# w_out's and w_ch's pieces decoded as one sequence, v's copies issued by ScalarE, x's rows stored two ticks later, and attention's state sums as one scan

## The chip, the cores and the metric

The kernel runs on one core of one Trainium2 chip. The metric is the device time of one execution in microseconds, the median of three runs. In the profile PE is TensorE (its weight loads are PEld), DVE is VectorE, ACT is ScalarE, POOL is GpSimd and SP is SyncE, which issues nearly all DMAs of this kernel.

## What is computed

A retention block (attention with a decay in place of the softmax), a block with a spatial gate, and a channel block follow one another. Cut to what matters:

```python
# q, k, v: (4, 8, 576, 64)
rel = pos[:, None] - pos[None, :]
Dmat = np.where(rel >= 0, gamma[:, None, None] ** rel[None, :, :], 0.0)
x = np.matmul(scale * np.matmul(q, k.transpose(0, 1, 3, 2)) * Dmat, v)   # heads side by side: (4, 576, 512)

h = gelu(x @ w_in)                                     # tanh form; w_in (512, 1024)
u, v = h[..., :512], h[..., 512:]
v_n = (v - mean(v)) / np.sqrt(var(v) + 1e-06) * g_ln
v_s = np.einsum('ts,bsd->btd', w_sg, v_n) + b_sg[None, :, None]
y = x + (u * v_s) @ w_out

xn = (y - mean(y)) / np.sqrt(var(y) + 1e-06) * g_ln2
out = y + np.maximum(xn @ w_ch1, 0.0) @ w_ch2          # w_ch1 (512, 2048), w_ch2 (2048, 512)
```

w_in, w_out and w_ch arrive as float64 words and are turned into float32 on the chip.

## The kernel before

The program is written out in one order; each engine carries out its own instructions in that order, and waits for the others by semaphores. Three stages follow one another.

**Attention** works on sixteen units, one for each of 4 batches and 4 pairs of heads, and is linear in the sequence: it is cut into four chunks of 128 positions and a rest of 64. For a unit, `scores` makes the products of q and k within the chunks (L224) and VectorE masks them (L229, L237); `states` (L239) makes a 64x64 state for each chunk and head (L245), side by side in one PSUM bank `us`, and sums them with decay: y of chunk c is y of chunk c - 1 times a factor per partition, plus the state. ScalarE copies chunk 0 (L251), and VectorE adds the other three one after another (L253). `attend` multiplies the masked scores with v (L277) and the summed states with q (L284, L290), with y as the stationary operand, and VectorE scales the result into `xb` (L295, L300). The loop (L453) puts scores and states of unit n + 1 ahead of attend of unit n. The tables of masks and decays, `tab`, one for each pair of heads, hold 451 columns and are loaded by SyncE between the first units; the factor is one column of it, at O_GC.

**Decoding in the background.** `f64_pieces` (L349) turns a list of 512-word pieces into float32. It loads two pieces ahead; then each piece takes four steps: a third load and a shift on VectorE (L142); the next VectorE instruction (L146), and the split of the piece before by ScalarE and GpSimd (L310, L311); a square on ScalarE (L148) and a VectorE instruction (L149); and the last VectorE instruction (L151), which waits for that square, with a store (L376) for w_ch. The steps are called by hand, `background(n)` for n steps: three in each attention unit from the third on, and then by the table `PACE`, so many after each tile. `background_steps` (L417) strings w_in, w_sg, w_out and most of w_ch together. w_out and w_ch are two calls of `f64_pieces`, so between them stands one step of its own: the last split of w_out and the first two loads of w_ch. By the counts of the table it is the second of three steps behind the first u chunk of batch 0.

**The gated stage** runs batch by batch. For each batch: `v_tile` makes 128 rows of v (in batches 0 and 2 also a tile numbered 4 that holds the rests of two batches), `u_chunk` four chunks of u in two halves, `sg_chunk` the spatial product with w_sg, whose five products over rows take v's tiles 0, 1, 2, 3 and the rest in this order, and `w_out_tile` the last product. Each evacuation by GELU on ScalarE (L529) is a tick, as is each half of the spatial product and each output tile. `after(n, fn)` puts work n ticks later into the program. So a tile of v is normalized in pieces over four ticks: mean and squares (L513, L514), variance and root (L498, L499), three small VectorE instructions (L519, L521, L523), and in the fourth the normalization on ScalarE (L526) with the split into high and low parts by ScalarE (L554) and GpSimd (L555). For the tile with the two rests, the fourth tick has DMAs in place of the split: two copy its lower half into `v_rest` (L587), a third puts the upper half over the lower (L588), and the split comes three ticks later. SyncE issues them. In batch 0 that fourth tick is the first half of the first u chunk, and tile 3's three small instructions come in the first half of the second. The splits of tiles 1, 2, the rests and 3 follow in this order.

Ahead of each u chunk, `turn_x` (L665) transposes 128 rows of x on VectorE into a tile of the pool `t` (five slots, shared with v's tiles and the rows that come back) and at once stores it with four DMAs on SyncE (L676); a fifth, shorter one comes ahead of the spatial product. `load_x` reads the rows back for the output tiles.

**The channel stage** (from L971 on) is a fast matrix product by blocks; it and the transformation of its weights are as they were.

Of the kernel before, what the change touches and what calls it, by code (L numbers as in the profile page):

```python
# [3 lines left out]

# [1 line left out]

# [5 lines left out]
F32 = mybir.dt.float32  # L12
# [3 lines left out]
ALU = mybir.AluOpType  # L16
# [3 lines left out]
B, H, S, D = 4, 8, 576, 64  # L20
E = H * D
NP = H // 2
F1 = 1024
F2 = 2048
C = 128
NC = S // C
R = S - NC * C
KE = E // 128
NF = F2 // 128
# [17 lines left out]
LATE = 6  # L47
# [15 lines left out]
O_GROW = O_MASKR + R  # L63
O_GK = O_GROW + C
O_GC = O_GK + 2
TA = O_GC + 1


O_GLN = 0
# [5 lines left out]
def const_tables():  # L75
    g = np.array(GAMMA, np.float64)
    p = np.arange(128)
    tab = np.zeros((NP, 128, TA), np.float64)
    for hp in range(NP):
        for h in range(2):  # L80
            gh = g[2 * hp + h]
            tab[hp, :, O_MASK + h * C:O_MASK + (h + 1) * C] = (np.arange(C)[None, :] >= p[:, None]) * gh ** -p[:, None]
            tab[hp, :, O_GK + h] = gh ** (C - p)
        gp = g[2 * hp + p // D][:, None]
        tab[hp, :, O_MASKR:O_MASKR + R] = (np.arange(R)[None, :] >= (p % R)[:, None]) * gp ** -(p % R)[:, None]
        tab[hp, :, O_GROW:O_GROW + C] = gp ** np.arange(C)[None, :] / np.sqrt(D)
        tab[hp, :, O_GC] = gp[:, 0] ** C
    return tab.astype(np.float32)


# [1 line left out]
def kernel(  # L92
# [12 lines left out]
    nc = tc.nc  # L105
    ctx.enter_context(tc.manual_schedule())
    act, dve, pool, pe = nc.scalar, nc.vector, nc.gpsimd, nc.tensor
# [12 lines left out]
    def col(t, o, n=1):  # L120
        return t[:, o:o + n]
# [9 lines left out]
    def f64_words(src, n):  # L131

        raw = f64_at[0].tile([128, n, 2], U32, tag="raw", name="raw")
        nc.sync.dma_start(out=raw.rearrange("p n w -> p (n w)"), in_=src.bitcast(U32))
        return raw

    def f64_to_f32(raw, n):


        c = f64_at[1].tile([128, n], U32, tag="c", name="c")  # L140
        w0, w1 = raw[:, :, 0], raw[:, :, 1]
        dve.tensor_scalar(  # L142
            out=c, in0=w1, scalar1=3, scalar2=0x3FFFFFFF, op0=ALU.logical_shift_left, op1=ALU.bitwise_and
        )
        yield
        dve.scalar_tensor_tensor(out=c, in0=w1, scalar=0xC0000000, in1=c, op0=ALU.bitwise_and, op1=ALU.bitwise_or)  # L146
        yield
        act.activation(out=f(w1), in_=f(w1), func=ACTF.Square)  # L148
        dve.scalar_tensor_tensor(out=c, in0=w0, scalar=29, in1=c, op0=ALU.logical_shift_right, op1=ALU.bitwise_or)  # L149
        yield  # L150
        dve.scalar_tensor_tensor(  # L151
            out=f(c), in0=f(w1), scalar=F64_LEAST ** 2, in1=f(c), op0=ALU.is_ge, op1=ALU.mult
        )
        return f(c)
# [4 lines left out]
    def bank():  # L159

        return banks.popleft()
# [3 lines left out]
    def slot(name):  # L165
        return wts.tile([128, 4 * 512], F32R, tag="w", bufs=9, name=name)
# [7 lines left out]
    pa = es_a.enter_context(tc.tile_pool(name="pa", bufs=2))  # L174

    tab = [pa.tile([128, TA], F32, tag=f"tab{hp}", bufs=1, name=f"tab{hp}") for hp in range(NP)]

# [61 lines left out]
    def states(n):  # L239
        u = units[n]  # L240
        us = bank()
        for c in range(NC):
            for h in range(2):
                r = slice(h * D, (h + 1) * D)
                pe.matmul(  # L245
                    us[r, c * D:(c + 1) * D], u["k"][:, c, r],
                    u["v"][:, c * C + h * D:c * C + (h + 1) * D], start=True, stop=True,
                )

        y = u["y"] = pa.tile([128, NC, D], F32, tag="y", name="y")  # L250
        act.copy(y[:, 0], us[:, 0:D])  # L251
        for c in range(1, NC):
            dve.scalar_tensor_tensor(  # L253
                out=y[:, c], in0=y[:, c - 1], scalar=col(tab[n % NP], O_GC), in1=us[:, c * D:(c + 1) * D],
                op0=ALU.mult, op1=ALU.add,
            )
        free(us)

    def attend_rest(n):
# [49 lines left out]
    def split(hi, lo, src):  # L309
        act.copy(hi, src)  # L310
        pool.tensor_tensor(out=lo, in0=src, in1=f(hi), op=ALU.subtract)  # L311

    def load_w_in():
        for k in range(KE):
            t = slot("w_in").rearrange("p (a n) -> p a n", a=2)
            wi.append(t)
            for x in range(0, F1, 512):
                c = slice(x, x + 512)
                yield (w_in[k, :, c], t[:, 0, c], t[:, 1, c])

    def load_w_out():
        for k in range(KE):
            if k % 2 == 0:
                s = slot("w_out").rearrange("p (k a n) -> p k a n", k=2, a=2)
            t = s[:, k % 2]
            wo.append(t)
            yield (w_out[k], t[:, 0], t[:, 1])
# [21 lines left out]
    def f64_pieces(pieces, lead=2):  # L349

        pieces = iter(pieces)
        ahead = deque()

        def load():
            todo = next(pieces, None)
            if todo is not None:
                ahead.append((todo, f64_words(todo[0], 512)))

        for _ in range(lead):
            load()  # L360
        yield
        before = None
        while ahead:
            load()
            todo, raw = ahead.popleft()
            steps = f64_to_f32(raw, 512)
            next(steps)
            yield
            if before is not None:
                split(*before)  # L370
                before = None
            c = yield from steps
            if len(todo) == 3:
                before = (todo[1], todo[2], c)
            else:
                nc.sync.dma_start(out=todo[1], in_=c)  # L376
            yield
        if before is not None:
            split(*before)
# [35 lines left out]
    w_ch_pieces = decode_w_ch()  # L415

    def background_steps():  # L417
        yield from f64_pieces(load_w_in(), 1)
        yield from load_w_sg()
        yield from f64_pieces(load_w_out())  # L420
        yield from f64_pieces(islice(w_ch_pieces, 2 * NF - LATE))

    bg = background_steps()

# [114 lines left out]
    def after(n, fn):  # L539
        late.append((step[0] + n, fn))  # L540
# [16 lines left out]
    def v_tile(b, i, ps=None):  # L557

        if ps is None:
            ps = v_products(b, i)  # L560
        if i == 0:
            vn[b] = tuple(big.tile([128, NC + 1, 512], F32R, tag=f"vn{a}", name=f"vn{a}") for a in "hl")
            if b % 2:
                after(1, lambda: iter([split_v(b, NC, v_rest[b])]))
        t = t1.tile([128, 512], F32, tag="t", bufs=NBT, name="t")

        st = numbers(t1)

        def norm_t():
            yield from squares(st, t, vn[b][0][:, i])  # L570

            def numbers_t():
                root(st, st[:, 1:2], 1.0 / 512, 1e-6)
                yield

            after(1, numbers_t)
            after(2, lambda: newton(st))

            def rest():
                normed(t, st)  # L580
                if i < NC:
                    split_v(b, i, t)
                else:

                    r = v_rest[b + 1] = t1.tile([128, 512], F32, tag="rest", bufs=1, name="v_rest")
                    for h in range(2):
                        nc.sync.dma_start(out=r[h * R:(h + 1) * R], in_=t[R:])  # L587
                    nc.sync.dma_start(out=t[R:], in_=t[0:R])  # L588
                    after(3, lambda: iter([split_v(b, i, t)]))
                yield  # L590

            after(3, rest)

        gelu(t, ps, ps, norm_t, st[:, 0:1])
        background(int(PACE[b][0][i]))
# [69 lines left out]
    def turn_x(b, i):  # L665

        n = 128 if i < NC else R
        t = t1.tile([128, 512], F32, tag="t", bufs=NBT, name="x_t")[:, 0:4 * n]
        dve.transpose(  # L669
            out=t.rearrange("p (q k c) -> p k q c", k=KE, c=32),  # L670
            in_=xb[b][:, :, i * 128:i * 128 + n].rearrange("p k (q c) -> p k q c", c=32),
        )
        at = 0 if i < NC else b % 2 * R
        to = x_dram[y_rows.index((b if i < NC else b | 1, i)), at:at + n]
        for q in range(4):
            nc.sync.dma_start(  # L676
                out=to[:, q * 128:(q + 1) * 128].rearrange("(a j) c -> j a c", j=32),
                in_=t[q * 32:(q + 1) * 32].rearrange("j (a c) -> j a c", c=128),
            )

    def load_x(b, i):
        x_rows[b, i] = t1.tile([128, E], F32, tag="t", bufs=NBT, name="x_r")
# [152 lines left out]
    for b in range(B):  # L835
# [27 lines left out]
        if last:  # L863
            for _ in bg:
                pass
            t = [wts.tile([128, KE * (S + R)], F32R, tag="xt", bufs=2, name="fe") for _ in range(2)]
            u = [slot("fe") for _ in range(4)]
# [36 lines left out]
        if last:  # L904
            next(feat)
            w1_at = [[slot("w1") for _ in range(2)]]
            t = slot("w2").rearrange("p (i a n) -> p i a n", i=2, a=2)
# [254 lines left out]
```

## Time and profile before

| | before |
|---|---|
| median of 3 runs | 700.74 us (699.19 to 702.92) |
| profiled execution: time, span | 702.03 us, 700.2 us |
| TensorE busy | 668.7 us (96%) |
| VectorE busy | 482.9 us (69%) |
| ScalarE busy | 303.2 us (43%) |
| GpSimd busy | 341.7 us (49%) |
| TensorE's granted clock, mean | 0.986 |
| DMA | 116.96 MB, mean 167 GB/s |

The span reaches from the first to the last instruction; the profiled execution's own time is 1.8 us more. Busy times are shares of the whole span and say nothing of a stage: attention lies in the first 90 us, the gated stage between 85 and 330 us, the channel stage behind it. A matmul is pipelined, so that the busy time of TensorE counts overlapped matmuls once. [...]

### The profile page before, as it was taken

How to read it: one execution, taken by the hardware profiler on the slowest of the kernel's cores; microseconds unless marked ns; L12 is line 12 of the kernel's file. 1: busy time of each engine (PE TensorE's matmuls, PEld its weight loads, DVE VectorE, ACT ScalarE, POOL GpSimd, SP SyncE). 2: the span in 40 equal slices, each digit the busy share in tenths (PEclk: the TensorE clock that was granted, in tenths of full speed). 3: DMA queues.
4: the chain of work that ended last, by engine and by line, in shares of the span. 5: the costliest groups of instructions: out<-in, count | busy, mean ns of one | idle time of the engine just before them, and what ended most of it. 6: DMA issues, size and time to landing. Idle time of an engine off the chain costs nothing.

```text
span 700.2 us, 11668 instructions
## 1 busy us (share of the span) xinstructions
PE 668.7 (96%) x4294; PEld 594.4 (85%) x4294; DVE 482.9 (69%) x925; ACT 303.2 (43%) x584; POOL 341.7 (49%) x302
## 2 busy tenths in 40 slices
PE   6977997999999899999999999999999999999997
PEld 4866787989889789989888888888988888898985
DVE  2899775987997987686888676677656654433333
ACT  2344475345446436543444544343535433232221
POOL 0222445633622642993555498445448854445411
PEclk8999998999999999999999999999999999999999
DMA  8898635586596749535465523552641153121132
GB/s 323 288 353 301 201 108 161 155 277 198 167 306 206 226 153 259 161 129 208 166 181 169 147 76 106 186 164 93 190 122 61 64 189 124 61 97 69 30 121 90
DMA packets 61960, 116.96 MB, mean 167 GB/s; under 512 B 6480, under 2 KB 25936, under 8 KB 59984
## 3 DMA queue, kind: packets, MB, share of 16 engines
q1 hardware_dynamic: 61904, 116.23, 51.5%
q8 instruction: 33, 0.54, 0.3%
q14 instruction: 23, 0.19, 0.1%
HBM read 88.16 MB, written 27.26 MB: 165 GB/s over the span
## 4 chain that ended last, share of the span: by engine, by line
PE 55%; DVE 22%; DMA 7%; ACT 7%; issue 5%; POOL 3%; SPq 1%; DVEq 0%; ACTq 0%; POOLq 0%
PE b L124 16%; PE b L126 16%; PE b L125 16%; PE b L698 4%; DVE c L151 2%; DVE c L142 2%; DVE c L149 2%; DVE c L146 2%; DVE p L229 2%; DMA w_dram<-c 1%; DMA ld<-in_attn_dram 1%; DVE y L253 1%; DMA rows<-y_dram 1%; DVE xb L295 1%; DVE x_t L669 1%
## 5 line engine op out<-in xcount | busy, mean ns | idle before, releaser
L124 PE MATMUL b<-fe,w 128*128 128x384 f32 x336 | 114.6, 341 | 1.9 <-DVE h L967 1.1
L766 POOL TENSOR_TENSOR w<-raw_w,w 128x512 fp32r<-128x512 f32 x46 | 62.4, 1356 | 107.3 <-ACT w L765 104.3
L126 PE MATMUL b<-w,h 128*128 128x512 f32 x288 | 114.2, 396 | 0.0
L124 PE MATMUL b<-w,h 128*128 128x512 f32 x288 | 113.7, 395 | 0.0
L125 PE MATMUL b<-w,h 128*128 128x512 f32 x288 | 113.5, 394 | 0.0
L125 PE MATMUL b<-fe,w 128*128 128x384 f32 x336 | 113.3, 337 | 0.0
L126 PE MATMUL b<-fe,w 128*128 128x384 f32 x336 | 113.1, 337 | 0.0
L966 ACT ACTIVATE h<-b 128x384 fp32r<-128x384 f32 x72 | 35.3, 490 | 160.4 <-DVE b L994 122.2
L967 DVE SCALAR_TENSOR_TENSOR h<-b,h 128x384 fp32r<-128x384 f32 x72 | 40.0, 556 | 45.6 <-ACT h L966 45.6
L124 PEld LDWEIGHTS b<-fe,w 128*128 128x128 f32 x336 | 63.0, 188 | 9.5 <-DVE t L989 2.7
L752 POOL TENSOR_TENSOR w<-raw_w,w 128x768 fp32r<-128x768 f32 x23 | 45.8, 1993 | 48.3 <-ACT w L751 44.5
L125 PEld LDWEIGHTS b<-fe,w 128*128 128x128 f32 x336 | 63.1, 188 | 3.6
L126 PEld LDWEIGHTS b<-w,h 128*128 128x128 f32 x288 | 54.1, 188 | 13.1
L126 PEld LDWEIGHTS b<-fe,w 128*128 128x128 f32 x336 | 63.1, 188 | 0.0
L125 PEld LDWEIGHTS b<-w,h 128*128 128x128 f32 x288 | 54.1, 188 | 9.4
L124 PEld LDWEIGHTS b<-w,h 128*128 128x128 f32 x288 | 54.0, 188 | 8.7
L148 ACT ACTIVATE raw<-raw 128x512 f32<-128x512 f32 x44 | 29.9, 680 | 64.1 <-DVE c L146 58.9
L994 DVE TENSOR_TENSOR b<-b,u 128x384 f32<-128x384 f32 x48 | 26.9, 561 | 39.7 <-PE b L126 39.6
L751 ACT CAST w<-raw_w 128x1024 fp32r<-128x1024 f32 (+1 forms) x47 | 44.2, 943 | 12.7 <-POOL raw_w L742 8.0
L499 POOL TENSOR_TENSOR st<-st,par 128x1 f32<-128x1 f32 x36 | 23.0, 640 | 52.4 <-DVE st L498 52.1
L389 POOL TENSOR_TENSOR xt_lo<-xb,xt_hi 128x576 fp32r<-128x576 f32 x16 | 25.0, 1575 | 45.6 <-ACT xt_hi L388 41.4
L752 DVE TENSOR_TENSOR w<-raw_w,w 128x1024 fp32r<-128x1024 f32 x24 | 35.4, 1477 | 13.8 <-ACT w L751 13.8
(140 smaller groups left out, 1619.3 us busy)
## 6 DMA issues: line engine op xcount, KB each, us to landing
ld<-in_attn_dram SPq DMA_DIRECT2D x15, 1120.0 KB, 7.1
raw<-in_w_ch_dram SPq DMA_DIRECT2D x32, 512.0 KB, 4.9
raw_w<-w_dram SPq DMA_DIRECT2D x24, 512.0 KB, 3.8
raw_w<-w_dram SPq DMA_DIRECT2D x46, 256.0 KB, 2.6
w_dram<-c SPq DMA_DIRECT2D x32, 256.0 KB, 2.5
row<-y_dram SPq DMA_DIRECT2D x30, 256.0 KB, 4.4
x_r<-x_dram SPq DMA_DIRECT2D x18, 256.0 KB, 4.4
y_dram<-x_r SPq DMA_DIRECT2D x18, 256.0 KB, 3.0
```

The costliest lines, as they stand in the source:

```text
L124: pe.matmul(ps, lh, rh, start=first, stop=False, skip_group_check=True)
L125: pe.matmul(ps, lh, rl, start=False, stop=False, skip_group_check=True)
L126: pe.matmul(ps, ll, rh, start=False, stop=last, skip_group_check=True)
L148: act.activation(out=f(w1), in_=f(w1), func=ACTF.Square)
L389: pool.tensor_tensor(out=lo[:, k, 0:S], in0=xb[b][:, k], in1=f(hi[:, k, 0:S]), op=ALU.subtract)
L698: pe.matmul(ps, g, wo[k][:, w], start=done[0] == 1, stop=done[0] == 3 * KE, skip_group_check=True)
L751: act.copy(hi, r)
L752: (pool if s and part else dve).tensor_tensor(out=lo, in0=r, in1=f(hi), op=ALU.subtract)
L766: pool.tensor_tensor(out=t[:, 1], in0=raw, in1=f(t[:, 0]), op=ALU.subtract)
L966: act.activation(out=t[:, 0], in_=v, func=ACTF.Relu)
L967: dve.scalar_tensor_tensor(out=t[:, 1], in0=v, scalar=0.0, in1=f(t[:, 0]), op0=ALU.max, op1=ALU.subtract)
L994: dve.tensor_tensor(out=v, in0=v, in1=u, op=ALU.add)
```

## The change

Four edits.

1. `states` writes the four chunk states interleaved: element e of chunk c goes to column 4 e + c, where it went to column 64 c + e. One scan on VectorE then goes over all 256 columns: each result is the one before times the table's factor, plus the state. The table holds a column for each of the 256 elements, zero at each chunk 0, so that a sum starts anew there. ScalarE's copy is gone. `u["y"]` is a view of the result with a step of four.
2. `background_steps` hands w_out's and w_ch's pieces to one call of `f64_pieces`. The step between them is gone.
3. v's three copies are issued by ScalarE.
4. `turn_x` puts its four stores two ticks later.

```diff
-TA = O_GC + 1
+TA = O_GC + NC * D
...
-        tab[hp, :, O_GC] = gp[:, 0] ** C
+        tab[hp, :, O_GC:] = gp ** C * (np.arange(NC * D)[None, :] % NC > 0)
...
         us = bank()
+        us_c = us[:, 0:NC * D].rearrange("p (e c) -> p c e", c=NC)
         for c in range(NC):
             for h in range(2):
                 r = slice(h * D, (h + 1) * D)
                 pe.matmul(
-                    us[r, c * D:(c + 1) * D], u["k"][:, c, r],
+                    us_c[r, c], u["k"][:, c, r],
                     u["v"][:, c * C + h * D:c * C + (h + 1) * D], start=True, stop=True,
                 )
 
-        y = u["y"] = pa.tile([128, NC, D], F32, tag="y", name="y")
-        act.copy(y[:, 0], us[:, 0:D])
-        for c in range(1, NC):
-            dve.scalar_tensor_tensor(
-                out=y[:, c], in0=y[:, c - 1], scalar=col(tab[n % NP], O_GC), in1=us[:, c * D:(c + 1) * D],
-                op0=ALU.mult, op1=ALU.add,
-            )
+
+        y = pa.tile([128, D * NC], F32, tag="y", name="y")
+        u["y"] = y.rearrange("p (e c) -> p c e", c=NC)
+        dve.tensor_tensor_scan(
+            out=y, data0=col(tab[n % NP], O_GC, NC * D), data1=us[:, 0:NC * D], initial=0.0, op0=ALU.mult, op1=ALU.add
+        )
         free(us)
...
-        yield from f64_pieces(load_w_out())
-        yield from f64_pieces(islice(w_ch_pieces, 2 * NF - LATE))
+        yield from f64_pieces(chain(load_w_out(), islice(w_ch_pieces, 2 * NF - LATE)))
...
                     for h in range(2):
-                        nc.sync.dma_start(out=r[h * R:(h + 1) * R], in_=t[R:])
-                    nc.sync.dma_start(out=t[R:], in_=t[0:R])
+                        act.dma_start(out=r[h * R:(h + 1) * R], in_=t[R:])
+                    act.dma_start(out=t[R:], in_=t[0:R])
                     after(3, lambda: iter([split_v(b, i, t)]))
...
-        for q in range(4):
-            nc.sync.dma_start(
-                out=to[:, q * 128:(q + 1) * 128].rearrange("(a j) c -> j a c", j=32),
-                in_=t[q * 32:(q + 1) * 32].rearrange("j (a c) -> j a c", c=128),
-            )
+
+        def store():
+            for q in range(4):
+                nc.sync.dma_start(
+                    out=to[:, q * 128:(q + 1) * 128].rearrange("(a j) c -> j a c", j=32),
+                    in_=t[q * 32:(q + 1) * 32].rearrange("j (a c) -> j a c", c=128),
+                )
+            yield
+
+
+        after(2, store)
```

## Rows read from the trace of the kernel before

**Rows 1.** Engines' busy us (instructions) in three stretches, granted clock, DMA share, GB/s

```profile
10.00:15.00 5.00, 3.28 (x39) 2.83 (x38) 1.30 (x4) 1.06 (x4) 0.00 (x0) 0.71 1.02 419
...
50.00:75.00 25.00, 20.86 (x370) 18.01 (x365) 24.34 (x56) 9.45 (x22) 5.82 (x5) 1.00 0.81 288
...
121.00:122.00 1.00, 1.00 (x6) 1.00 (x6) 1.00 (x2) 0.00 (x0) 0.00 (x0) 0.50 0.53 199
```

**Rows 2.** VectorE's timeline in attention: start us, duration us, instruction, [idle before it]

```profile
26.71 0.91 DVE L253 SCALAR_TENSOR_TENSOR y<-y,tab,b 128x64 f32<-128x64 f32 x3
...
63.29 0.91 DVE L253 SCALAR_TENSOR_TENSOR y<-y,tab,b 128x64 f32<-128x64 f32 x3
64.12 0.68 DVE L295 TENSOR_TENSOR xb<-b,tab 128x512 f32<-128x512 f32 x1
64.72 0.21 DVE L300 TENSOR_TENSOR xb<-b,tab 128x64 f32<-128x64 f32 x1
64.85 0.68 DVE L151 SCALAR_TENSOR_TENSOR c<-raw,c 128x512 f32<-128x512 f32 x1
...
77.82 0.91 DVE L253 SCALAR_TENSOR_TENSOR y<-y,tab,b 128x64 f32<-128x64 f32 x3
```

**Rows 3.** Chain that ended last: start, us, what; load, unit, copies

```profile
3.19 9.20 DMA ld<-in_attn_dram
...
80.89 1.09 PE b L224 x16
...
82.36 0.61 PE b L245 x16
...
83.85 0.80 PE b L284 x12
...
84.66 0.11 PE b L290 x4
...
107.86 0.55 SPq L587
...
108.85 2.23 DMA v_rest<-t
...
111.22 2.19 DMA t<-t
```

**Rows 4.** TensorE's timeline at its waits in batches 0, 1 and 2

```profile
118.76 0.61 PE L124 MATMUL b<-w_sg,vnh 128*128 128x288 f32 x1 [3.84 <-ACT vnh L554]
...
120.12 0.61 PE L126 MATMUL b<-w_sg,vnl 128*128 128x288 f32 x1 [0.51 <-POOL vnl L555]
...
124.60 0.36 PE L125 MATMUL b<-w_sg,vnh 128*128 128x288 f32 x1
...
173.37 0.40 PE L126 MATMUL b<-w_sg,vnl 128*128 128x288 f32 x1 [0.89 <-POOL vnl L555]
...
191.68 1.66 PE L698 MATMUL b<-w_out,glh 128*128 128x512 f32 x6 [1.00 <-ACT glh L645]
...
233.36 0.40 PE L126 MATMUL b<-w_sg,vnl 128*128 128x288 f32 x1 [1.38 <-POOL vnl L555]
```

**Rows 5.** ScalarE's timeline in batches 0, 1 and 2

```profile
106.72 0.80 ACT L526 ACTIVATE t<-t,st 128x512 f32<-128x512 f32 x1
...
108.56 0.62 ACT L554 CAST vnh<-t 128x512 fp32r<-128x512 f32 x1
...
190.45 0.68 ACT L148 ACTIVATE raw<-raw 128x512 f32<-128x512 f32 x1 [3.01 <-issue]
...
225.84 0.62 ACT L554 CAST vnh<-t 128x512 fp32r<-128x512 f32 x1
```

**Rows 6.** VectorE's timeline in batches 0 and 1

```profile
115.67 0.43 DVE L142 TENSOR_SCALAR c<-raw 128x512 uint32<-128x512 uint32 x1 [7.49 <-DMA raw<-in_w_ch_dram]
...
167.00 1.32 DVE L151 SCALAR_TENSOR_TENSOR c<-raw,c 128x512 f32<-128x512 f32 x1 [0.95 <-ACT raw L148]
```

**Rows 7.** GpSimd's timeline in batch 0

```profile
118.79 1.28 POOL L555 TENSOR_TENSOR vnl<-t,vnh 128x512 fp32r<-128x512 f32 x1 [3.39 <-ACT vnh L554]
```

More of the change, by code (lines that the diff above doesn't have):

```diff
@@ L2 @@
 from contextlib import ExitStack
-from itertools import islice
+from itertools import chain, islice
 import numpy as np
```

## The prediction

> **What bounds the kernel now.** I read three views in this order: the busy times by stretch, the chain of waits, and then the timelines of single engines at the places where the chain leaves TensorE. In attention (sixteen units of work) VectorE is the bound: from 50 to 75 us it is busy 24.34 of 25 us while TensorE is busy 20.86 [rows 1]. From about 79 us to the end TensorE runs without a gap, except at a few places. Those that this change touches are the first spatial product of batches 0, 1 and 2, and one wait later in batch 1 [rows 4]. So three questions decide: what an attention unit costs on VectorE, when those products get their operands, and whether anything pushes TensorE over VectorE in attention. Times of VectorE, ScalarE and GpSimd elsewhere cost nothing.
>
> **Part 1, the scan.** Today a unit's state sums are one ScalarE copy and three dependent VectorE instructions of 64 elements (L253). From the start of the three to the start of the next instruction pass 64.12 − 63.29 = 0.83 us [rows 2]. They become one scan over 256 elements. The trace holds no scan. Its neighbours: 512 elements from PSUM step on after 64.72 − 64.12 = 0.60 us, 64 elements after 64.85 − 64.72 = 0.13 us [rows 2], so 256 elements at that pace would be 0.13 + 192 × (0.47/448) = 0.33 us. Each element of a scan needs the one before, as each of today's three instructions does, so the other end is what those cost, 0.83 us, no gain at all. I take 0.60 us, two such steps per element, nearly the middle: a gain of 0.23 us a unit. It counts only where VectorE is the bound: eleven units, from the sums at 26.71 to those at 77.82 [rows 2]; the later ones start when TensorE already has a backlog. 11 × 0.23 = 2.5 us (ends 0 and 5.5).
>
> [...]
>
> The ScalarE copy (L251) that goes was waited for by VectorE only before and after the bound stretch, so its removal is worth nothing on the path.
>
> The table of each head pair grows from 451 to 706 columns, 255 × 4 × 128 bytes = 131 kB. Two of these tables are loaded ahead of unit 1, whose load is the first link of the chain and lands at 12.39 us [rows 3]. At the 419 GB/s of that stretch [rows 1] that is 0.6 us later, all on the path. Attention: 2.5 − 0.6 = **1.9 us gained** (−0.6 to 4.9 by the scan's ends).
>
> The same edit makes TensorE write the states with a step of four words and read the sums back with a step of four as stationary operand. TensorE's own work for a unit is 84.66 + 0.11 − 80.89 = 3.88 us in the chain, of it 0.61 us for the states and 0.80 + 0.11 us for the products that use the sums [rows 3]. VectorE's unit takes (77.82 − 26.71)/10 = 5.1 us [rows 2], and 4.9 afterwards, so about 1.0 us more on TensorE is hidden. No row has a stepped operand; I take no cost, since the cover is two thirds of the 1.52 us concerned. The cost above that is a rival below.
>
> **Part 2, one sequence of pieces.** Between w_out's last and w_ch's first piece there is today one step that only starts two loads. It falls in batch 0's first u chunk, and the very next step needs the first of these loads: VectorE sits 7.49 us in front of L142 until 115.67 [rows 6]. Behind it in VectorE's queue wait a transpose and the last three small instructions that normalize v's tile 3; ScalarE and GpSimd then need until 120.07 [rows 7] to split that tile, and TensorE waits 3.84 and 0.51 us [rows 4]. [...] As one sequence, the loads run two pieces ahead and that wait goes. What would be late next is the tile of v whose rows are copied by DMA: it lands at 111.22 + 2.19 = 113.41 us [rows 3], and ScalarE casts it before tile 3. By cast, normalization, cast and subtraction (0.62 + 0.80 + 0.62 + 1.28 us, from [rows 5, 7]) tile 3 would then be ready at 116.7, 3.4 us sooner than 120.07. That is the worth of part 2 in batch 0 if part 3 cost nothing.
>
> It also moves every later decoding step one place forward. In batch 1, VectorE's L151 stands 0.95 us waiting for ScalarE's square [rows 6], in front of tile 3's normalization, and TensorE then waits 0.89 us for that tile [rows 4]; the square is now issued one call earlier, so I take 0.9 us (0 to 1.05). Later ScalarE's square at 190.45 waits for VectorE and holds back the cast of g behind it [rows 5], for which TensorE waits 1.00 us [rows 4]; with the step before it done one call sooner this goes too: 1.0 us (0 to 1.0). Batch 1: **1.9 us gained**. Other calls hold as many steps as before and TensorE waits for none of them.
>
> **Part 3, v's copies on ScalarE.** Two copies are issued behind the normalization that ends at 106.72 + 0.80 = 107.52 [rows 5], then a third that overwrites what the first two read and so waits until they have landed. SyncE does this today: it issues from 107.86, at 0.55 us for an issue, the copies land at 108.85 + 2.23 = 111.08, the third is issued at 111.22 [rows 3]. SyncE had little behind it but the loads of part 2. ScalarE has its whole queue: the evacuations of u, and the normalizations and casts of v's tiles 1, 2 and 3. If ScalarE waits as SyncE did, it is held for 111.22 − 107.86 = 3.36 us and the third issue, some 3.8 us, from 107.52 to 111.3 (2.2 us, the landing alone, is the lower end). The cast of tile 1 at 108.56 [rows 5] slides to 112.4 and ends at 113.0; GpSimd then has five subtractions of 1.29 us [rows 7] in a row (tile 1, w_out, tile 2, the copied tile, tile 3), up to 113.0 + 5 × 1.3 = 119.5. TensorE's last wait in batch 0 ends at 119.6, not 120.12 [rows 4]: of the 3.4 us only **0.5 us** stay (up to 2.0 with the short hold). Since TensorE idles as long, I leave its clock as it is.
>
> Batch 2 has the same copies but no load in the way. TensorE's last wait there ends at 233.36 [rows 4]. The cast of tile 1 at 225.84 [rows 5] slides by 3.5 us to 229.4 and ends at 230.0; four subtractions give 235.2, 1.8 us later than now. VectorE too is held, as it waits in order for a row that ScalarE normalizes in that queue, which makes up to 3.2 us. I take 2.4 us: **2.4 us lost** (0.7 to 3.2).
>
> **Part 4, x's stores.** Four DMA issues per tile move behind two evacuations, but stay ahead of the loads and stores of the decoding call that follows, so on SyncE they pass only rows and z of the third stage, and, in batches 0 and 2, v's copies, which leave that queue. Each holds its slot of five a little longer. No wait in the path ends with them: 0 (a loss of up to 0.9 us if a transpose waits for the slot, the size of the wait in batch 1 [rows 4]).
>
> **Sum.** 1.9 + 0.5 + 1.9 − 2.4 + 0 = 1.9 us off 702.03 us of the profiled execution, 700.1 us. That execution is 1.3 us above the median, 700.74, so the forecast is **698.8 us**; by the unknown ends of the parts 695 to 702.
>
> **Rivals.**
> - The scan streams like any two-operand instruction, 0.33 us: 3.0 us more, 695.8 us. For it speaks that nothing in the rows is slower than one element a step; against it the dependence from element to element.
> - ScalarE is not held: the copies run beside its work, or its delay falls into slack. Then batch 0 gives 3.4 us instead of 0.5 and, TensorE idling for less than half as long, the low clock goes too, half of the 4.5 us from 120.12 to 124.60 [rows 4]; batch 2 loses nothing. That is 2.9 + 2.2 + 2.4 = 7.5 us below the forecast, 691.3 us. Against it speaks that ScalarE's queue is full just there: its rows of batch 0 have no idle time before them [rows 5].
> - Slower: the stepped operands. The place is TensorE in every attention unit; it decides from 1.0 us a unit on. At twice the time for the states and the products with the sums (1.52 us more) a unit takes 5.4 us on TensorE, against 5.1 on VectorE now: eleven times 0.3 lost in place of 2.5 gained, 704.6 us; at three times, 721 us. For it: L245 and L284 are short and many. Against it: their share is covered up to 1.0 us. [...]
> - Part 2's shift does nothing in batch 1, because something else ends those waits: 700.7 us, within the bound.
>
> **How the numbers follow.** Forecast 0.42, free-running scan 0.16, ScalarE not held 0.15, stepped operands 0.15, no gain in batch 1 0.12. The range leaves out the lower half of the second rival and the upper half of the third: 691 to 705. A measurement of this kernel can tell about 0.5%, 3.5 us: below 697.2 lie most of the first two rivals and the lower edge of the forecast, 0.35; above 704.2 the stepped operands, 0.14; the rest 0.51.
>
> **What would show it.** Right: one VectorE instruction of about 0.68 us per unit in place of three; no wait for w_ch's load before L142; ScalarE empty for 3 to 4 us after the normalization in batches 0 and 2, ended by a DMA; TensorE still waiting at both first spatial products, and no longer 1.00 us in batch 1. Wrong: TensorE's busy time in attention up by more than a quarter, ScalarE running through the copies, or the clock at full speed after batch 0's wait.

## The result, and the profile after

The changed kernel takes 705.34 us (median, 704.36 to 708.29), the kernel before 700.29 us on the same chip: a ratio of 1.0077 with a 95% interval of 1.006 to 1.0093. It is 5 us slower, where 1.9 us faster was forecast, and just above the forecast range. The profiled execution has 704.62 us and a span of 702.7 us.

First the busy times by stretch of the kernel after (length, TensorE, its weight loads, VectorE, ScalarE, GpSimd, granted clock as a share of full speed, DMA share, GB/s); the first line answers to [rows 1]:

```profile
50.00:75.00 25.00, 22.25 (x376) 19.46 (x374) 24.72 (x49) 11.71 (x24) 7.27 (x6) 1.00 0.82 305
100.00:125.00 25.00, 20.18 (x119) 18.43 (x118) 14.55 (x34) 12.62 (x25) 9.88 (x10) 0.80 0.49 131
225.00:250.00 25.00, 18.50 (x101) 17.14 (x102) 21.50 (x32) 13.23 (x26) 15.66 (x12) 0.73 0.47 139
```

The same view of before, in the two stretches of the spatial products of batches 0 and 2:

```profile
100.00:125.00 25.00, 20.66 (x133) 19.92 (x132) 14.11 (x35) 15.06 (x31) 11.65 (x11) 0.86 0.46 137
225.00:250.00 25.00, 21.88 (x145) 20.90 (x143) 24.27 (x38) 12.99 (x27) 15.51 (x14) 0.93 0.69 202
```

Attention is still bound by VectorE, busy for 24.72 of 25 us. The losses are the two stretches below it: in both, TensorE is busy for less time and at a lower granted clock, and above all in batch 2.

VectorE's timeline in attention, against [rows 2]: one scan of 0.68 us, after which the next instruction starts 0.60 us on.

```profile
72.00 0.68 DVE L254 TENSOR_TENSOR_SCAN y<-tab,b 128x256 f32<-128x256 f32 x1
72.60 0.67 DVE L295 TENSOR_TENSOR xb<-b,tab 128x512 f32<-128x512 f32 x1
```

The chain of waits (start, us, what), against [rows 3]: TensorE's unit, the first product of v, which marks the end of the attention stretch (78.99 us, 84.77 before), and in batch 0 the copies.

```profile
74.93 1.09 PE b L224 x16
...
76.40 0.61 PE b L246 x16
...
77.89 0.91 PE b L284 x12
78.81 0.19 PE b L290 x4
78.99 0.43 PE b L124
...
102.52 5.55 DMA v_rest<-t
```

ScalarE in batch 0, against [rows 5]. Its DMA issues (ACTq) stand among its instructions, and from 101.94 to 108.68 it carries out nothing else, 6.74 us:

```profile
101.14 0.80 ACT L525 ACTIVATE t<-t,st 128x512 f32<-128x512 f32 x1
101.97 1.15 ACTq L586 DMA_DIRECT2D v_rest<-t  x2
108.16 0.47 ACTq L587 DMA_DIRECT2D t<-t  x1
108.68 0.41 ACT L528 ACTIVATE u<-b 128x288 f32<-128x288 f32 x1 [6.74 <-DMA x_dram<-x_t]
```

(The releaser named there, a store of x, is not what ScalarE waited for: the third copy is issued as soon as v_rest has landed, at 102.52 + 5.55 = 108.07 us.) In batch 2 the same, for 4.05 us:

```profile
221.20 1.13 ACTq L586 DMA_DIRECT2D v_rest<-t  x2
224.71 0.47 ACTq L587 DMA_DIRECT2D t<-t  x1
225.22 0.41 ACT L528 ACTIVATE u<-b 128x288 f32<-128x288 f32 x1 [4.05 <-DMA v_rest<-t]
```

TensorE's waits, against [rows 4], for batches 0, 1 and 2 (five in batch 0, two in batch 1, four in batch 2):

```profile
110.49 0.40 PE L124 MATMUL b<-w_sg,vnh 128*128 128x288 f32 x1 [1.95 <-ACT vnh L553]
111.84 0.61 PE L126 MATMUL b<-w_sg,vnl 128*128 128x288 f32 x1 [0.82 <-POOL vnl L554]
...
116.75 0.61 PE L126 MATMUL b<-w_sg,vnl 128*128 128x288 f32 x1 [1.05 <-POOL vnl L554]
...
190.70 0.73 PE L703 MATMUL b<-w_out,glh 128*128 128x512 f32 x2 [1.21 <-ACT glh L644]
...
227.74 0.61 PE L124 MATMUL b<-w_sg,vnh 128*128 128x288 f32 x1 [2.97 <-ACT vnh L553]
229.57 0.61 PE L126 MATMUL b<-w_sg,vnl 128*128 128x288 f32 x1 [0.98 <-POOL vnl L554]
...
233.54 0.61 PE L124 MATMUL b<-w_sg,vnh 128*128 128x288 f32 x1 [2.13 <-ACT vnh L553]
234.89 0.61 PE L126 MATMUL b<-w_sg,vnl 128*128 128x288 f32 x1 [0.50 <-POOL vnl L554]
```

The waits of batch 0 come to 4.8 us, 4.4 before; those of batch 2 to 6.6 us, 3.1 before. They now come one by one, with single products at the low clock between them (0.50 from 112 to 113 us). In batches 0 and 2 together the waits grew by 3.9 us; the stretches grew by 8.9 us (table below), and the rest, 5.0 us, is products that come more slowly.

**A table by stage.** All kernels here run the same products, so one number per batch says what its operands' lateness costs: the time from the first spatial product with w_sg to the end of the last but two, from TensorE's timeline (the two products of the rests that close each batch, 0.26 us, are left out). Without a wait and at full clock it is 14.75 us (batch 3 of before, granted clock 1.00 from 282 to 298 us). "First v" is the start of the first product of v after attention in the same timeline (0.07 us ahead of the chain's). All in us; the kernels are those of the next section.

| kernel | time | against before | first v | batch 0 | batch 1 | batch 2 |
|---|---|---|---|---|---|---|
| before | 700.29 | | 84.70 | 22.0 | 16.3 | 20.2 |
| after | 705.34 | +5.1 | 78.92 | 24.3 | 15.1 | 26.8 |
| e1, copies on SyncE | 696.33 | -4.6 | 80.27 | 16.1 | 15.5 | 21.0 |
| e2, scan alone | 698.67 | -2.3 | 81.17 | 21.5 | 16.6 | 21.5 |
| e3, one sequence alone | 698.67 | -2.3 | 82.81 | 16.5 | 16.1 | 23.1 |
| e4, copies on ScalarE alone | 708.08 | +7.1 | 81.74 | 24.1 | 16.7 | 25.8 |
| e5, third copy on SyncE | 699.49 | -1.4 | 79.71 | 20.8 | 16.0 | 23.4 |
| e6, third copy two ticks on | 701.86 | +0.9 | 78.95 | 22.0 | 15.3 | 24.0 |
| e7, no third copy | 696.86 | -4.1 | 79.93 | 18.8 | 15.3 | 23.7 |
| e8, stores at once | 706.60 | +5.7 | 78.95 | 23.7 | 15.4 | 26.1 |
| e9, e3 and a step given back | 695.73 | -5.2 | 82.25 | 16.5 | 14.9 | 20.0 |
| e10, e1 and a step given back | 692.03 | -8.9 | 78.77 | 16.2 | 16.0 | 20.8 |
| e11, loads on ScalarE too | 705.73 | +5.8 | 79.87 | 22.0 | 15.5 | 27.1 |

"Against before" is the difference to before's median on the same chip (699.97 to 700.94). Each stretch and each "first v" is from one execution; those of e6, e8 and e9 are 2 to 3 us below the medians of their kernels.

### The profile page after: what moved, and what is told of

The parts are those of the page before. It is cut to its first block, busy times and chain, and to the rows that moved or that the text cites. A ratio compares the mean times of both kernels' runs of the same rounds, so it can differ in the third digit from the quotient of the medians.

```text
span 702.7 us, 11609 instructions
## 1 busy us (share of the span) xinstructions
PE 674.5 (96%) x4294; PEld 598.2 (85%) x4294; DVE 477.3 (68%) x893; ACT 301.4 (43%) x568; POOL 343.2 (49%) x302
## 3 DMA queue, kind: packets, MB, share of 16 engines
q1 hardware_dynamic: 61424, 115.97, 50.8%
## 4 chain that ended last, share of the span: by engine, by line
PE 63%; DVE 16%; DMA 7%; ACT 5%; POOL 4%; issue 3%; SPq 1%; ACTq 0%; DVEq 0%; POOLq 0%
PE b L124 18%; PE b L126 18%; PE b L125 18%; PE b L703 4%; DMA ld<-in_attn_dram 2%; DVE c L146 2%; DVE c L149 2%; DVE c L151 2%; DMA w_dram<-c 2%; DVE p L229 1%; DMA v_rest<-t 1%; POOL vnl L554 1%; DVE c L142 1%; POOL xt_lo L389 1%; DVE h L972 1%
## 5 line engine op out<-in xcount | busy, mean ns | idle before, releaser
L126 PE MATMUL b<-w,h 128*128 128x512 f32 x288 | 114.2, 397 | 0.0
L124 PE MATMUL b<-w_sg,vnh 128*128 128x288 f32 x128 | 41.0, 321 | 7.3 <-ACT vnh L553 7.3
L151 DVE SCALAR_TENSOR_TENSOR c<-raw,c 128x512 f32<-128x512 f32 x44 | 38.2, 869 | 14.1 <-ACT raw L148 11.9
L498 POOL TENSOR_TENSOR st<-st,par 128x1 f32<-128x1 f32 x36 | 23.4, 651 | 49.6 <-DVE st L497 49.3
```

The lines of the kernel that those rows point to most:

```text
L124: pe.matmul(ps, lh, rh, start=first, stop=False, skip_group_check=True)
L126: pe.matmul(ps, ll, rh, start=False, stop=last, skip_group_check=True)
L151: dve.scalar_tensor_tensor(out=f(c), in0=f(w1), scalar=F64_LEAST ** 2, in1=f(c), op0=ALU.is_ge, op1=ALU.mult)
```

## The experiments

### Part by part: e1 to e4

Theory A: ScalarE, held at its copies, is the loss. Theory B: the loss lies in the other edits. e1 is the changed kernel with the copies back on SyncE; e2, e3 and e4 are before with one edit each (the lines of the diff ahead of the prediction).

```diff
 # e1, on the changed kernel
-                        act.dma_start(out=r[h * R:(h + 1) * R], in_=t[R:])
-                    act.dma_start(out=t[R:], in_=t[0:R])
+                        nc.sync.dma_start(out=r[h * R:(h + 1) * R], in_=t[R:])
+                    nc.sync.dma_start(out=t[R:], in_=t[0:R])
```

> The changed kernel with v's three copies per even batch issued by SyncE again; scan, one sequence and later stores stay. Theory A (ScalarE, held at its copies, is the loss): in the trace of the changed kernel ScalarE is empty for 6.7 us in batch 0 and 4.1 us in batch 2, and the waits of the first spatial products with the half clock behind them come to some 2.4 us more than before in batch 0 and some 6 in batch 2; without the hold both should fall to before's or below, and the 5.8 us that attention ends earlier should stay: 692 to 698 us, ScalarE without a gap of over 3 us ahead of tile 3's normalization. Theory B (the loss comes from the scan, the sequence or the stores: attention that ends earlier meets other transfers and weights that are not there): the time stays at 703 to 706, with the same waits at the first spatial products.

> Before with the scan and its bigger table alone. Theory A: attention ends 3.5 us earlier for 15 units at 0.23 us each, and up to 2.1 more or less by which decoding steps fall onto GpSimd's work; batch 0 may keep its wait for a w_ch piece, which has less time to arrive, and give back up to 3 of it: 695 to 699 us. Theory B (what attention gains is lost again at batch 0's first spatial product): 699 to 702, attention's end near 79 to 81 us instead of 84.8 and the wait at the first spatial product longer than 3.8 us.

> Before with one sequence of decoded pieces alone. My prediction put this at 3.4 us in batch 0 (VectorE no longer waits 7.5 us for the load of a piece ahead of tile 3's numbers) and 1.9 in batch 1: by Theory A 695 to 698 us. Rival: the piece's load leaves at the same moment behind SyncE's copies, or another tile is late next: 699 to 701.

> Before with the copies issued by ScalarE alone. Theory A (the hold is the loss by itself): ScalarE held for 4 to 7 us in batches 0 and 2, but batch 0's first spatial product waits for VectorE's numbers in any case: 702 to 707 us, most of the loss in batch 2. Rival (the hold only hurts once the w_ch wait is gone): 699 to 702 us, since SyncE is free to send the w_ch loads that stood behind the copies.

Ratios to before: e1 0.9937 (0.9921 to 0.9952), e2 0.9967 (0.9954 to 0.9980), e3 0.9968 (0.9954 to 0.9981), e4 1.0101 (1.0085 to 1.0117). Theory A holds: the scan and the sequence gain 2.3 us each and together, with the later stores, 4.6 (e1), so that for the stores nothing is left. The copies cost 7.1 us alone and 5.1 + 4.6 = 9.7 us beside the other edits. The single edits therefore add up to only 2.5 us of loss, half of the result. Where the copies cost more beside the others the table shows: batch 0 grows by 2.1 us with the copies alone, where VectorE still waits 4.48 us for w_ch's load in front of L142 (7.49 before, [rows 6]), and by 8.2 us from e1 to the changed kernel, where that wait is gone. The times of e3 and e4 lie 0.7 and 1.1 us above the ranges that theory A gave them.

In e2 batch 0's waits are nearly before's (3.84 and 0.51 us, [rows 4]), so attention's gain is passed on there; of the 3.5 us by which attention ends earlier in its execution, batches 1 and 2 take back 1.6 us:

```profile
115.27 0.61 PE L124 MATMUL b<-w_sg,vnh 128*128 128x288 f32 x1 [3.70 <-ACT vnh L554]
116.63 0.61 PE L126 MATMUL b<-w_sg,vnl 128*128 128x288 f32 x1 [0.51 <-POOL vnl L555]
```

In e3 the wait of 3.84 us is gone from batch 0 and only two short ones stay (0.41 and 0.82 us), but new ones stand in batch 2, and in batch 1 the wait of 1.00 us ahead of a product with w_out (191.68 in [rows 4]) has shrunk to 0.22 us, but a later one of these products now waits 1.22 us:

```profile
114.81 0.40 PE L126 MATMUL b<-w_sg,vnl 128*128 128x288 f32 x1 [0.82 <-POOL vnl L554]
...
189.04 0.73 PE L697 MATMUL b<-w_out,glh 128*128 128x512 f32 x2 [1.22 <-ACT glh L644]
...
224.97 0.40 PE L126 MATMUL b<-w_sg,vnl 128*128 128x288 f32 x1 [1.29 <-POOL vnl L554]
...
228.11 0.40 PE L124 MATMUL b<-w_sg,vnh 128*128 128x288 f32 x1 [1.50 <-ACT vnh L553]
```

The table shows the exchange: batch 0 5.5 us shorter, batch 2 2.9 longer.

In e4 ScalarE is held for 6.32 us in batch 0 and 3.89 in batch 2, although nothing else was changed:

```profile
104.60 1.14 ACTq L587 DMA_DIRECT2D v_rest<-t  x2
110.38 0.47 ACTq L588 DMA_DIRECT2D t<-t  x1
110.90 0.41 ACT L529 ACTIVATE u<-b 128x288 f32<-128x288 f32 x1 [6.32 <-PE b L126]
```

### What of the copies costs: e5 to e8

Theory A1: the wait ahead of the third copy. Rival A2: the second queue, on which the copies land late.

```diff
 # e5
-                    act.dma_start(out=t[R:], in_=t[0:R])
+                    nc.sync.dma_start(out=t[R:], in_=t[0:R])
 # e6
-                    act.dma_start(out=t[R:], in_=t[0:R])
-                    after(3, lambda: iter([split_v(b, i, t)]))
+                    def third():
+                        act.dma_start(out=t[R:], in_=t[0:R])
+                        yield
+                    after(2, third)
+                    after(4, lambda: iter([split_v(b, i, t)]))
 # e7, with the copies into v_rest on SyncE; in split_v for tile 4 of batches 0 and 2
+            for h in range(2):
+                act.copy(vh[h * R:(h + 1) * R, i], t[0:R])
+            for h in range(2):
+                pool.tensor_tensor(out=vl[h * R:(h + 1) * R, i], in0=t[0:R], in1=f(vh[0:R, i]), op=ALU.subtract)
 # e8: the four stores of turn_x at once, as before
```

> The changed kernel with only the third copy (t's own rows, which has to wait for the two before it) issued by SyncE; ScalarE still issues the two copies into v_rest. Theory A1 (ScalarE loses what it waits at the third copy, 5.0 us of the 6.7 in batch 0 and 2.4 of the 4.1 in batch 2): ScalarE is out only for the two issues, 1.1 to 1.2 us each batch, and 7 of the 9 us that the copies on ScalarE cost come back: 697 to 699 us. Rival A2 (the copies on a second queue are the cost: they land after 5.6 us beside other transfers, where they took 2.3 us in SyncE's order, and tile 4's split comes late by that): v_rest still lands after 5 us, SyncE stands at the third copy instead with stores and loads behind it: 701 to 705.

> The changed kernel with ScalarE's third copy issued two ticks later and the split that needs it one tick later than it was. A tick is 1.6 us here (12 products of 0.13 us). A1: ScalarE has about 3.2 us of other work before it has to wait, so the 6.7 us of batch 0 fall to about 3.5 and the 4.1 of batch 2 to about 1, and over half of the 9 us come back: 698 to 701 us. A2: the landing is as late as before, the split too: 703 to 706.

> The changed kernel with the copies into v_rest on SyncE and no third copy: ScalarE and GpSimd write both halves of tile 4's parts from the same 64 rows, in two instructions each instead of one (0.6 us more on ScalarE, about 1.3 more on GpSimd in batches 0 and 2). Against the version with all copies on SyncE (696.3 us): ScalarE's waits for that copy, 1.2 us in batch 0 and 1.7 in batch 2, go, and GpSimd's 1.3 us come. Theory A: one of them is late next, 695 to 697 us. Rival: GpSimd's splits are the last thing that the first spatial products wait for (3.4 us in all there), so its second instruction stands in the path: 697 to 699.

> The changed kernel with x's stores issued at once again; all else as changed. My prediction had the later stores at nothing, with a loss of at most 0.9: 704 to 706 us. Rival (the later stores fall beside the copies and make them land late): v_rest lands after 2 to 3 us in batch 0 instead of 5.6 and the time falls to 700 to 702.

e5: 0.9981 (0.9962 to 0.9999), e6: 1.0010 (0.9994 to 1.0027). With no wait on ScalarE 6.5 of the 9.7 us come back (+5.1 to -1.4), with a shorter wait 4.2 (+5.1 to +0.9). Both times lie between the ranges of the two theories. e5 takes away the wait and, as the rows below show, the late landing too, so its two thirds are not A1's alone. What is left of the cost in e5 goes with the two issues, 1.15 us of ScalarE's time, since e5 and e1 differ in nothing else: its waits in batch 0 are 2.8 us, 0.8 in e1, and behind them TensorE runs at the low clock (0.50) from 114.2 to 119.0 us; in e1 the clock is 1.00 from 118 to 119 us.

The two also show A2's half truth. In e6 SyncE sent a w_ch load at 102.69 us, just behind the copies, and they landed only at 107.9; ScalarE still waits 2.61 us:

```profile
107.88 0.47 ACTq L588 DMA_DIRECT2D t<-t  x1
108.39 0.81 ACT L525 ACTIVATE t<-t,st 128x512 f32<-128x512 f32 x1 [2.61 <-DMA x_dram<-x_t]
```

In e5 SyncE stands at the third copy, so the load leaves behind it, and both batches' copies land after 2.3 to 3.0 us:

```profile
106.14 0.55 SPq L587 DMA_DIRECT2D t<-t  x1
106.75 2.03 SPq L677 DMA_DIRECT2D x_dram<-x_t  x4
108.88 0.37 SPq L134 DMA_DIRECT2D raw<-in_w_ch_dram  x1
```

e7: 0.9944 (0.9931 to 0.9958), as e1 within the two intervals. Taking ScalarE's waits for that copy away gains nothing. The stretches of batches 0 and 2 are each 2.7 us longer than e1's in these two executions, and other places are shorter, among them the ways from the end of batch 0's stretch to that of batch 1's (49.9 us, 51.4 in e1) and from batch 2's to batch 3's (49.3, 51.0); why, I did not follow. e8: 1.0083 (1.0061 to 1.0105), as the changed kernel within the two intervals, and 0.6 us above the range expected. The later stores cost nothing and are not why the copies land late.

### Does the load make the copies late: e11

```diff
+        q = act if src.tensor is w_ch.tensor else nc.sync
-        nc.sync.dma_start(out=raw.rearrange("p n w -> p (n w)"), in_=src.bitcast(U32))
+        q.dma_start(out=raw.rearrange("p n w -> p (n w)"), in_=src.bitcast(U32))
```

> The changed kernel with w_ch's loads (512 KB each) issued by ScalarE too, so that in batch 0 they stand behind v's copies in one program order, as they stood in SyncE's before. Theory C (the copies land late, after 5.2 to 5.6 us where they took 2.2 to 3.0, because a w_ch load runs beside them): in batch 0 they land after 2.2 to 3.0 us again and ScalarE is out for about 4 us instead of 6.7, as in batch 2; with 0.4 to 0.5 us on ScalarE for each load issue the time is 701 to 705 us. Rival D (copies issued by ScalarE land late by themselves, or behind x's stores): 5 us or more again, and 705 to 708 us.

The landing went as theory C has it. The chain of waits:

```profile
103.45 2.41 DMA v_rest<-t
```

SyncE sent four of x's stores just ahead (101.31 to 103.10) and four more from 105.29, as the changed kernel does from 100.37 and 105.22. What is missing beside the copies is the load, so it is the load and not the stores that made 2.41 us into 5.55. ScalarE is out for 3.54 us in batch 0, and its stretch is 22.0 us, before's. The time did not follow, 1.0087 (1.0070 to 1.0103), and lies in rival D's range: batches 1 and 2 are 0.4 and 0.3 us longer than after (in batch 2 ScalarE is out for 4.56 us), attention ended 1 us later in this execution, and the load issues now cost ScalarE 0.35 us each (its busy rows don't count them). I did not take these apart.

### Where the sequence's gain goes: e9 and e10

With one sequence every later decoding step stands one place ahead. e9 and e10 have one step fewer ahead of batch 1, so that from there on each stands where it was before.

```diff
-    ("13233", "3432", "2220", "34333"),
+    ("13233", "3432", "2220", "24333"),
```

> Before with one sequence of pieces, and with one decoding step fewer at the first w_out tile of batch 0, so that from batch 1 on each decoding step stands where it stood before the change. One sequence alone made batch 0 5.5 us shorter in its trace and the stretch from batch 1's last spatial product to batch 2's 3.9 us longer. Theory P (the decoding steps' new places cost batch 2 what they gave batch 0): batches 1 and 2 return to before's 51.2 and 61.5 us between their last spatial products, batch 0 keeps its 5.5: 695 to 697 us, against 698.7 without the step given back. Rival Q (batch 2's loss has nothing to do with the steps' places, but with the attention and loads ahead of it, or it differs from run to run): batch 2 stays near 65 us and the time at 698 to 700.

> The changed kernel with the copies on SyncE (696.3 us) and the same decoding step fewer at batch 0's first w_out tile. P: batch 2, 63.3 us there, returns to 61.5 and batch 1 stays: 694 to 696 us. Q: 696 to 697.5.

e9: 0.9928 (0.9912 to 0.9943), e10: 0.9891 (0.9870 to 0.9912). Theory P holds for batch 2: 3 us come back in e9, and the waits of batch 2 are before's to a hundredth (0.24, 1.50 and 1.38 us there; the last in [rows 4]):

```profile
221.25 0.40 PE L126 MATMUL b<-w_sg,vnl 128*128 128x288 f32 x1 [0.24 <-POOL vnl L554]
223.15 0.40 PE L124 MATMUL b<-w_sg,vnh 128*128 128x288 f32 x1 [1.50 <-ACT vnh L553]
225.06 0.61 PE L126 MATMUL b<-w_sg,vnl 128*128 128x288 f32 x1 [1.38 <-POOL vnl L554]
```

e10, the changed kernel with the copies on SyncE and one step moved, is the fastest, 8.9 us below before and 4.3 below e1, more than P had. From the end of batch 1's spatial product to the end of batch 2's its trace has 62.1 us (217.2 + 20.8 - 175.9) where e1's has 63.3, and from there to batch 3's 49.4 instead of 51.0; another 1.5 us is attention's earlier end in its execution. Batch 1 does not go by the places: with those of before, e9 has no wait in its spatial product and e10 one of 0.89 us, where before has 1.05 us in two.

## Why the prediction was wrong

| term | forecast | runs |
|---|---|---|
| scan | 1.9 gained | 2.3 gained (e2) |
| one sequence, without part 3 | 3.4 + 1.9 = 5.3 gained | 2.3 gained (e3) |
| copies on ScalarE | 2.9 + 2.4 = 5.3 lost | 7.1 lost alone (e4), 9.7 beside the rest |
| later stores | 0 | 0 (e8) |

Two steps failed. The larger is the cost of the copies on ScalarE: the prediction priced how much later the last operand comes and took the products in between at their old speed ("I leave its clock as it is"). From before to after, batches 0 and 2 together were to lose 2.4 - 0.5 = 1.9 us; their waits grew by 3.9 us, and slower products, which the sum had at nothing, took 5.0 us more. The other is the sequence behind batch 0, which was to gain 1.9 us and lost about 3.

**Part 1 was right.** The step of the scan is the 0.60 us that I took. The loss for the bigger tables does not show: the first load lands at 12.34 us, 12.39 before [rows 3]. VectorE's unit, from the fourth scan to the fourteenth, a tenth of the time, is 4.62 to 4.98 us in the nine profiles with the scan and 5.06 to 5.11 in the four without [rows 2]: 0.31 us less on average, where I had 0.23. The 5.8 us by which the two profiles above differ at the end of attention are more than the change: with the old sums the first product of v starts between 81.74 and 84.70 us in four profiles, with the scan between 78.77 and 81.17 in nine. The rival of the stepped operands fell. States with a step of four words take the same 0.61 us; reading the sums takes 0.91 + 0.19 us instead of 0.80 + 0.11, 0.2 us a unit, well under the cover of 1.0.

**Part 2 was right for batch 0 and wrong behind it.** With the copies on SyncE its wait falls to 1.2 us (e3), and the clock stays at the full level (1.00 from 100 to 125 us, 0.86 before), so the gain is 5.5 us: 3.1 of waiting, where I had 3.4, and 2.4 of slow products, which I had only in a rival, with 2.2, an estimate from the clock of 0.50 in [rows 1]. The step that failed is "Other calls hold as many steps as before and TensorE waits for none of them". The calls hold as many steps, but other ones. In batch 2 TensorE waits longer with these, and e9 shows that their places alone took the 3 us. In batch 1 neither of the two gains came. VectorE's wait for the square is gone, as forecast, but in e3 TensorE waits 1.02 us in the spatial product, 1.05 before: GpSimd's last two subtractions now run beside VectorE's decoding and take 1.74 us each on average, where they took 1.28 and 1.35. The changed kernel has no wait there (its stretch falls from 16.3 to 15.1 us), but that is not the sequence's doing alone, and which edit does it stays open. From the end of batch 0's stretch to that of batch 1's e3 has 52.0 us, before 51.2, e1 51.4 and the changed kernel 49.7. The wait of 1.00 us at w_out's product [rows 4] did fall, to 0.17 us at 186.01 in the changed kernel, but 1.21 us stand at a later product, at 190.70: the call ahead of that product's cast of g now holds L151 and an L142 that takes 1.52 us beside GpSimd's work.

**Part 3 is the mis-sized term that decides.** The mechanism was forecast, and ScalarE's empty time was on the list of what would show it. The size was off in two places. The first is the sentence on batch 0 that begins "If ScalarE waits as SyncE did". ScalarE waited 6.7 us, not 3.8, because SyncE's own order had kept the w_ch load behind the copies. SyncE's timeline before:

```profile
107.86 1.46 SPq L587 DMA_DIRECT2D v_rest<-t  x2
111.22 0.46 SPq L588 DMA_DIRECT2D t<-t  x1
111.73 1.53 SPq L134 DMA_DIRECT2D raw<-in_w_ch_dram  x3
```

Once SyncE had only loads and stores, it sent the load of 512 KB at 102.67 us, and the copies, issued at 101.97, ran beside it. From 102.5 to 108.1 us the DMAs of SyncE's queue, that load among them, took 64.7% of the 16 DMA engines' time and those of ScalarE's, the copies, 17.7%; before, from 108.85 to 111.10 us, the copies' queue moved nothing else and took 50.8%. SyncE's timeline after:

```profile
100.37 2.01 SPq L677 DMA_DIRECT2D x_dram<-x_t  x4
102.67 0.35 SPq L134 DMA_DIRECT2D raw<-in_w_ch_dram  x1
```

In the nine kernels in which that load leaves behind the copies (before, e1, e2, e3, e5, e7, e9, e10, e11) they land after 2.2 to 3.5 us in both batches; in the four with the load beside them (after, e4, e6, e8) after 5.2 to 5.5 in batch 0. I had read the order of SyncE's queue as a fact about the copies' speed. With a hold of 3.5 us (e11) batch 0 is 22.0 us long, as before: about the "0.5 gained" that I had put for 3.8, and its last wait ends 115.04 - 108.93 = 6.1 us after the first spatial product, as forecast.

The changed kernel passes its longer hold on in full: counted the same way, TensorE's last wait was to end after 119.6 - 113.58 = 6.0 us and ends after 116.75 - 107.98 = 8.8, 2.8 us later, for a hold that is 2.9 us longer.

The second place is the clock, and batch 2 shows it best. There the hold was 4.05 us, near my 3.5, yet its stretch grew from 21.0 (e1) to 26.8 us, 5.8 lost where I took 2.4 and at most 3.2. I had followed the last wait alone. The waits grew by 2.8 us, close to the 2.4; the other 3.0 us are slower products. With the waits taken out, 34 of the stretch's 112 products start over 0.2 us after the one before them, 19 in e1 and 19 before, at a granted clock of 0.73 for the 25 us (0.93 in both).

## What to carry to other kernels

A DMA that waited for another one held the engine that issues it: SyncE from 107.86 us to the third issue at 111.22 before, ScalarE for 6.74 us in batch 0 of the changed kernel. Of the 6.74 the landing of the first two is 5.55 us and the issues are the rest; such a DMA belongs on an engine with nothing due. When DMAs leave a queue, ask what the queue will send in their place, because its order may have been keeping a large load off a small urgent copy: here the copies landed after 2.23 us ahead of the 512 KB load and after 5.55 us beside it. Taking one step out of a sequence written by hand moves every step behind it (batch 2 was 2.9 us longer in e3): look where each later one comes to stand, or give the step back at the next place that has slack. When an operand comes later, price the products behind the wait as well as the wait: from e1 to the changed kernel batch 2's waits grew by 2.8 us and its slower products by 3.0.

## What the runs showed of the hardware

VectorE and GpSimd took longer beside one another. In attention six of VectorE's decoding instructions in the profile before and five in that after take 0.1 to 1.2 us more than the others of their line, and each of them starts while GpSimd is at work. VectorE's timeline of before:

```profile
40.46 1.73 DVE L146 SCALAR_TENSOR_TENSOR c<-raw,c 128x512 uint32<-128x512 uint32 x1
42.22 0.69 DVE L149 SCALAR_TENSOR_TENSOR c<-raw,c 128x512 uint32<-128x512 uint32 x1
```

GpSimd's timeline of before:

```profile
40.37 1.27 POOL L311 TENSOR_TENSOR w_in<-c,w_in 128x512 fp32r<-128x512 f32 x1 [1.79 <-ACT w_in L310]
```

L146 ends at 42.19, 0.55 us after GpSimd's 41.64, which is nearly its usual 0.69 us: it seems to have done its work when GpSimd had done. The other ten end 0.27 to 0.28 us (L142, which otherwise takes 0.42) or 0.54 to 0.55 us after GpSimd's instruction. In the profile after, the decoding instructions that start ahead of GpSimd's, or less than 0.2 us before its end, take their usual time. The other way round, the subtraction of GpSimd at 163.33 us in the profile after takes 1.29 us, and the two from 165.00 on, beside VectorE's L146, L149 and L151, take 3.48 together. Which instructions meet differs between the two profiles, 2.3 us in all in the profile after and 4.3 before, which can be part of the spread of attention's end.

The low clock stands behind idle time of TensorE: in batch 0 after 1.95 us of waiting (after) or 3.84 (before) the products come every 0.24 us instead of every 0.13, at a granted clock of 0.50 (118 to 119 us after, 120 to 124 before). In e1, with one wait of 0.82 us in that batch, only a few products behind it and behind shorter gaps are that slow, and the granted clock is 1.00 from 112 to 113 and from 118 to 119 us. A later operand cost twice its own length in batch 2: from e1 to the changed kernel batch 2's waits grew by 2.8 us (3.7 to 6.6) and its stretch by 5.8.
